# Bucketed attention into a channel mix: row copies on GpSimd's queue, and one written sequence of operations

## The chip, the cores and the metric

The kernel runs on one core of a Trainium2 chip. A core has TensorE (PE in the profile; its weight loads are PEld), VectorE (DVE), ScalarE (ACT), GpSimd (POOL) and SyncE (SP). Each engine works through its own instructions in the order in which they stand in the program, and waits on semaphores for the others; SP here only issues DMAs, which run on 16 DMA engines. "SPq" and "POOLq" in the profile are DMA issues of those queues. The metric is the device time in microseconds, the median of several runs.

## The reference

Two stages follow each other. The first is attention in which a query sees only the keys of its own bucket: a bucket is the pattern of signs of six random projections. The second is a channel mix of the RWKV kind.

```python
batch, n_heads, seq, head_dim = (4, 8, 768, 64)
q_bits = (einsum('bhsd,dk->bhsk', q, proj) > 0)      # proj: 64 x 6
k_bits = (einsum('bhsd,dk->bhsk', k, proj) > 0)
mask = q_bucket[:, :, :, None] == k_bucket[:, :, None, :]
scores = where(mask, q @ k.T / sqrt(64), -1e9)
attn = softmax(scores); x = attn @ v                 # to (batch, 768, 512)
x_prev = x shifted by one position
xk = mu_k * x + (1 - mu_k) * x_prev                  # xr with mu_r
k = relu(xk @ w_k); v = (k * k) @ w_v                # 512 -> 1024 -> 512
out = sigmoid(xr @ w_r) * v
```

All inputs and the output are float32.

## The kernel before, in words

**Tiling.** Two heads make a pair, so there are 16 pairs, four to a batch; after each fourth pair the channel mix of that batch (numbered 0 to 3) can begin. A pair's Q and K are loaded (L485, L491), split by VectorE into an fp16 high part ("hi", L560) and low part ("lo", L563), both in the buffer nh, and transposed by DMA from SP into the operand tile a (L567). Pairs 0 and 1 are instead transposed on TensorE (L638) with evictions by VectorE and ScalarE (L643, L645), piece by piece.

**Bucket bits.** For pairs 1 to 15, TensorE multiplies the tile a with the projections (the "bits" group, 16 matmuls, L586), VectorE turns the signs into fp16 values of fixed size (bx, L589), and four DMAs copy six rows each (Q and K of both heads) back into the tile a, next to the 64 rows of data (L599). After that, one product of the K side and the Q side of a gives the score plus a constant for each bit in agreement, so the exponential of a pair in different buckets vanishes, and no mask is applied. A pair's scores therefore wait for its row copies. Pair 0 writes its bits in place (L668, L670).

**Scores to PV.** A pair has 9 score steps of 1024 columns (L702), each into one of three double banks of PSUM; ScalarE takes the exponential of each (L706). The bits group takes one of the same three double banks. PV is 12 matmuls at a time (L732); VectorE divides (L741 to L748), the result is transposed (L758 or by DMA, L764), and VectorE forms the mixed inputs xk and xr (L789 to L804). V is prepared by GpSimd: copies and sums (L511 to L523).

**Channel mix.** 16 groups with w_k (L822), ScalarE's relu (L826), VectorE's square (L829), 6 groups with w_r (L841) and a tanh (L844), 12 with w_v (L851), the product on VectorE (L858) and the store from SP (L861). w_k is loaded by four DMAs of GpSimd's queue (L446); w_r and w_v are loaded by SP and cast by GpSimd (L470).

**What sets the order.** All of it is added as 1328 operations to a planner (`Plan.add`, L124), each with engine, planned duration and the operations that it depends on. `Plan.schedule` (L159) plays this through in planned time: on each engine, of the operations that are ready, the one with the lowest entry in the list `WANT` (a wanted place for each operation) goes next; a large DMA is held back while the planned DMA work is more than `BACKLOG` ahead; the PSUM banks are given out first free first. What comes out is the fixed order of instructions on each engine; nothing of the plan remains at run time. `LAG` holds the planned time from an engine's end to when another can start.

Of the kernel before, what the change touches and what calls it, by code (L numbers as in the profile page):

```python
# [17 lines left out]
LAG = {"PE": 0.30, "ACT": 0.25, "DVE": 0.20, "POOL": 0.20, "SP": 1.8, "GQ": 2.0}  # L18


BACKLOG = 1.5

# [17 lines left out]
def R(kind, n):  # L40
# [3 lines left out]
WANT = [  # L44
    2, 8, 6, 12, 18, 10, 26, 38, 44, 24, 5, 11, 30, 34, 35, 23, 36, 3, 33, 14, 32, 22, 0, 9,
    25, 1, 39, 42, 45, 48, 49, 46, 59, 31, 112, 84, 74, 63, 101, 324, 348, 401, 425, 387, 414, 455, 482, 379,
    403, 446, 470, 4, 41, 13, 37, 102, 21, 7, 117, 47, 50, 52, 51, 65, 66, 53, 19, 58, 40, 54, 17, 68,
    71, 76, 80, 62, 67, 73, 77, 56, 82, 89, 95, 104, 98, 69, 15, 78, 83, 90, 103, 64, 75, 175, 115, 123,
    135, 133, 61, 57, 72, 87, 28, 27, 70, 60, 96, 86, 100, 79, 29, 20, 55, 16, 107, 110, 134, 120, 127, 119,
    106, 131, 43, 91, 99, 105, 81, 88, 118, 109, 122, 132, 113, 130, 125, 129, 97, 141, 144, 148, 121, 157, 159, 154,  # L50
    161, 155, 166, 167, 170, 176, 179, 181, 188, 185, 108, 85, 221, 137, 147, 152, 156, 94, 92, 128, 93, 126, 114, 158,
    169, 194, 174, 187, 173, 172, 145, 150, 163, 164, 171, 178, 162, 153, 168, 142, 146, 143, 160, 139, 151, 138, 140, 190,
    198, 197, 207, 208, 177, 195, 183, 180, 204, 237, 220, 230, 233, 246, 241, 192, 182, 281, 191, 196, 206, 210, 124, 136,
    149, 111, 116, 165, 186, 193, 227, 202, 228, 211, 214, 184, 257, 262, 231, 238, 239, 244, 219, 217, 226, 218, 189, 200,
    205, 216, 201, 199, 267, 268, 271, 274, 275, 234, 236, 242, 252, 253, 279, 288, 297, 305, 300, 311, 203, 229, 298, 240,
    245, 250, 255, 222, 224, 248, 209, 212, 235, 273, 277, 302, 286, 299, 294, 247, 256, 243, 249, 276, 285, 260, 265, 263,
    269, 283, 295, 251, 270, 278, 290, 225, 215, 315, 292, 280, 291, 318, 293, 296, 307, 319, 323, 330, 334, 338, 341, 345,
    349, 350, 357, 362, 374, 383, 393, 392, 420, 424, 428, 434, 437, 380, 386, 398, 417, 427, 435, 433, 441, 448, 495, 504,
    516, 413, 423, 429, 431, 449, 454, 452, 461, 468, 450, 527, 533, 439, 444, 459, 500, 507, 522, 512, 519, 541, 520, 536,
    539, 485, 492, 525, 546, 550, 597, 497, 514, 558, 563, 566, 607, 542, 560, 562, 567, 572, 638, 578, 586, 594, 649, 616,  # L60
    939, 530, 581, 625, 635, 650, 925, 656, 664, 613, 642, 686, 913, 266, 213, 356, 301, 308, 312, 322, 332, 327, 336, 232,
    223, 259, 254, 258, 272, 284, 304, 329, 328, 343, 316, 346, 352, 333, 344, 351, 360, 325, 335, 339, 408, 317, 331, 310,
    289, 313, 321, 303, 309, 402, 407, 405, 418, 421, 363, 367, 369, 372, 375, 340, 467, 494, 506, 502, 543, 503, 517, 337,
    365, 426, 314, 320, 326, 342, 355, 353, 361, 282, 287, 347, 261, 264, 306, 376, 381, 396, 404, 391, 412, 410, 416, 395,
    406, 399, 411, 359, 368, 422, 430, 388, 397, 354, 373, 384, 390, 370, 378, 471, 475, 508, 490, 524, 457, 462, 469, 473,
    478, 371, 599, 620, 626, 637, 641, 629, 639, 477, 364, 532, 377, 382, 385, 438, 440, 443, 463, 358, 366, 415, 389, 409,
    432, 481, 487, 509, 528, 501, 513, 515, 523, 419, 436, 442, 451, 488, 496, 505, 510, 445, 456, 460, 464, 465, 472, 476,
    480, 529, 535, 499, 545, 547, 583, 585, 593, 602, 606, 466, 612, 628, 633, 647, 655, 644, 678, 484, 511, 553, 447, 453,
    458, 474, 483, 479, 486, 498, 491, 518, 394, 400, 489, 551, 559, 574, 569, 584, 565, 549, 554, 538, 540, 557, 576, 651,
    659, 631, 654, 627, 634, 573, 592, 589, 600, 587, 596, 675, 679, 684, 691, 694, 660, 665, 668, 673, 683, 493, 706, 735,  # L70
    739, 743, 749, 746, 753, 808, 817, 825, 819, 828, 834, 788, 801, 810, 779, 787, 809, 827, 839, 848, 849, 857, 865, 833,
    843, 847, 872, 878, 884, 786, 852, 860, 876, 882, 887, 851, 861, 866, 886, 905, 902, 867, 871, 880, 906, 909, 916, 894,
    897, 901, 864, 908, 911, 783, 797, 923, 935, 953, 1003, 769, 784, 919, 940, 945, 952, 962, 968, 955, 966, 973, 995, 988,
    989, 1035, 1039, 1044, 1049, 999, 1005, 974, 992, 1010, 1017, 1048, 1057, 930, 949, 1061, 1063, 537, 580, 652, 548, 552, 556, 577,
    579, 582, 588, 521, 526, 561, 531, 534, 544, 617, 622, 657, 636, 630, 646, 610, 614, 671, 677, 666, 669, 619, 624, 621,
    632, 604, 609, 648, 653, 601, 605, 640, 645, 693, 713, 715, 718, 721, 688, 701, 704, 708, 710, 590, 772, 793, 794, 796,
    803, 800, 806, 570, 591, 643, 568, 571, 575, 663, 670, 667, 676, 555, 564, 623, 603, 611, 661, 705, 712, 737, 729, 750,
    725, 698, 702, 690, 695, 720, 722, 717, 723, 711, 714, 733, 741, 728, 731, 742, 748, 680, 687, 738, 744, 747, 757, 762,
    758, 752, 767, 771, 773, 681, 781, 812, 814, 821, 831, 818, 836, 618, 755, 917, 672, 682, 685, 696, 699, 703, 707, 595,
    598, 674, 608, 615, 692, 724, 730, 740, 760, 766, 778, 813, 820, 782, 792, 770, 776, 822, 829, 775, 790, 763, 768, 754,  # L80
    764, 751, 756, 761, 777, 856, 842, 841, 858, 862, 798, 802, 815, 823, 826, 709, 895, 915, 920, 921, 927, 924, 1054, 732,
    853, 824, 689, 697, 700, 719, 726, 727, 734, 658, 662, 716, 774, 780, 791, 859, 868, 881, 890, 873, 877, 830, 835, 845,
    850, 869, 874, 883, 891, 879, 885, 795, 804, 855, 863, 837, 846, 805, 811, 899, 918, 934, 937, 938, 893, 896, 898, 910,
    912, 736, 959, 976, 979, 981, 985, 1059, 1066, 1076, 1080, 1085, 1047, 1051, 1071, 1072, 1078, 1082, 1062, 1070, 1075, 1124, 1130, 1134,
    1084, 1090, 1101, 1087, 1093, 1098, 1095, 1108, 1115, 1135, 1141, 1144, 1064, 1106, 1111, 1086, 1100, 1104, 1092, 1120, 1123, 1149, 1156, 1158,
    1131, 1137, 1140, 1119, 1125, 1129, 1112, 1127, 1132, 1154, 1162, 1147, 1187, 1194, 1196, 1146, 1152, 1181, 1185, 1186, 1190, 1193, 1200, 1199,
    1206, 1208, 1211, 1217, 1221, 1161, 1170, 1223, 1227, 1224, 1229, 1232, 1238, 1242, 1246, 1220, 1226, 1235, 1234, 1240, 1243, 765, 807, 816,
    936, 941, 944, 961, 967, 970, 977, 759, 745, 844, 889, 892, 903, 943, 948, 965, 969, 956, 991, 947, 951, 926, 933, 900,
    904, 907, 914, 971, 975, 980, 984, 1004, 1009, 922, 928, 997, 1001, 1007, 1008, 1015, 1019, 1026, 1020, 1023, 1027, 1032, 1036, 983,
    1040, 1053, 1056, 1065, 1069, 1073, 1077, 799, 888, 986, 946, 950, 954, 990, 993, 996, 1000, 785, 789, 832, 838, 840, 854, 958,  # L90
    963, 972, 998, 982, 978, 1011, 1018, 987, 994, 1025, 1028, 1030, 1037, 1034, 1046, 1055, 1068, 1081, 1088, 1089, 1103, 1060, 1067, 1058,
    1094, 1107, 1113, 1117, 1122, 1126, 1128, 1133, 1136, 1002, 1139, 1153, 1155, 1157, 1160, 1159, 1163, 957, 960, 964, 1014, 1024, 1021, 1029,
    870, 875, 929, 931, 932, 942, 1097, 1099, 1105, 1116, 1102, 1110, 1045, 1052, 1013, 1022, 1050, 1074, 1118, 1121, 1091, 1096, 1142, 1145,
    1079, 1083, 1109, 1114, 1143, 1148, 1138, 1150, 1151, 1165, 1164, 1166, 1171, 1174, 1177, 1178, 1031, 1182, 1192, 1195, 1201, 1203, 1198, 1230,
    1006, 1012, 1016, 1033, 1038, 1041, 1042, 1184, 1189, 1197, 1202, 1191, 1188, 1180, 1183, 1173, 1175, 1204, 1207, 1168, 1172, 1176, 1179, 1169,
    1167, 1205, 1209, 1212, 1214, 1216, 1210, 1213, 1215, 1218, 1219, 1043, 1222, 1225, 1228, 1231, 1236, 1239, 1233, 1237, 1250, 1244, 1256, 1245,
    1249, 1251, 1255, 1260, 1262, 1248, 1252, 1254, 1261, 1266, 1268, 1258, 1263, 1265, 1264, 1269, 1271, 1253, 1257, 1259, 1278, 1283, 1286, 1273,
# [5 lines left out]

class Op:
    pass


class Plan:

    def __init__(self, pairs, banks, most, moe_most):
        self.ops = []
        self.writer = {}
# [39 lines left out]
    def schedule(self):  # L159
# [31 lines left out]
        t = 0.0  # L191
# [726 lines left out]
```

## Time and profile before

| | us |
|---|---|
| median of 3 runs (lowest to highest) | 254.8 (254.63 to 255.04) |
| span of the profiled execution, first to last instruction | 249.4 |
| lowest and highest run less that span (the page gives no time around the span) | 5.2 to 5.6 |
| TensorE / VectorE / ScalarE / GpSimd busy | 235.4 / 185.9 / 183.2 / 49.8 |
| first exponential, first matmul of the channel mix, end of TensorE's work | 12.7, 60.8, 245.6 |
| row copies on SP: number x median issue | 60 x 0.693 |

How to read it: a row of the stretches gives, for a window of time, the busy time of each engine in it with the number of instructions. In the order of time a row is a run of equal instructions, with their common length and, in brackets, the idle time of the engine ahead of it and what ended it. The chain of waits is followed back from the last instruction. A busy TensorE is not TensorE at its peak, since the ends of pipelined matmuls are modelled; start-to-start times of matmuls in a run say what they cost.

### The profile page before, as it was taken

What the parts mean: (1) busy time and instruction counts of PE and PEld (TensorE: products, weight loads), DVE (VectorE), ACT (ScalarE), POOL (GpSimd) and SP (SyncE); (2) the same over time, 40 slices, a digit from 0 to 9 for tenths busy, and PEclk for the clock granted to TensorE, in tenths of its full rate; (3) what the DMA queues carried; (4) which work ended last, traced back from release to release, by engine and by line L of the source; (5) the groups of instructions that cost most, each with busy time, mean ns of one, the idle gap of its engine ahead of it and who ended that gap; (6) DMA issues with size and microseconds to landing.
All of it is one profiled execution on the core that took longest, in us unless ns stands there. A gap on an engine that the chain in (4) does not pass through costs nothing.

```text
span 249.4 us, 6171 instructions
## 1 busy us (share of the span) xinstructions
PE 235.4 (94%) x2453; PEld 140.4 (56%) x2453; DVE 185.9 (75%) x415; ACT 183.2 (73%) x242; POOL 49.8 (20%) x89
## 2 busy tenths in 40 slices
PE   7897988897999999999999999999999999999993
PEld 3344654474667555558666666447666666555441
DVE  4997599899986987899989976786856626854321
ACT  3589859869999845899799988169997677247210
POOL 7209142245364123004100000522000000000000
PEclk9799999999999999999999999999999999999999
DMA  7994999998999999989968999945210103220123
GB/s 204 265 314 88 170 277 224 236 231 221 310 216 323 246 266 232 270 235 216 137 206 208 223 215 205 267 74 196 74 42 9 34 9 108 87 84 3 42 84 128
DMA packets 73341, 43.50 MB, mean 174 GB/s; under 512 B 55544, under 2 KB 68192, under 8 KB 73312
## 3 DMA queue, kind: packets, MB, share of 16 engines
q1 hardware_dynamic: 72656, 42.05, 68.8%
q0 software_dynamic: 576, 1.05, 2.3%
q8 instruction: 19, 0.31, 0.5%
q14 instruction: 10, 0.08, 0.1%
q10 hardware_dynamic: 80, 0.00, 0.0%
HBM read 24.12 MB, written 6.29 MB: 122 GB/s over the span
## 4 chain that ended last, share of the span: by engine, by line
PE 77%; DMA 7%; ACT 6%; DVE 3%; SPq 3%; issue 2%; DVEq 0%; ACTq 0%
PE ps_all L702 18%; PE ps_all L851 17%; PE ps_all L822 17%; PE ps_all L732 13%; PE ps_all L841 8%; ACT pt L706 6%; DMA nat<-in_k_dram 5%; PE ps_all L586 3%; DMA a<-bx 3%; SPq L599 2%; DVE bx L589 1%; SPq L567 1%; SPq L491 1%; DVE a L643 1%; DVE nh L625 0%
## 5 line engine op out<-in xcount | busy, mean ns | idle before, releaser
L706 ACT ACTIVATE pt<-ps_all 128x1024 bf16<-128x1024 f32 x144 | 140.6, 1042 | 24.0 <-PE ps_all L702 22.4
L702 PE MATMUL ps_all<-a 128*128 128x512 f16 (+1 forms) x384 | 81.3, 325 | 6.2 <-ACT pt L706 3.5
L702 PEld LDWEIGHTS <-a 128*128 128x128 f16 x384 | 33.6, 97 | 33.1 <-issue 10.4
L732 PEld LDWEIGHTS <-pt 128*128 128x128 bf16 x1152 | 43.6, 97 | 8.5 <-ACT pt L706 0.8
L822 PE MATMUL ps_all<-xk,wk 128*128 128x384 bf16 x256 | 47.4, 326 | 0.0
L851 PE MATMUL ps_all<-wv,k 128*128 128x512 bf16 x192 | 46.8, 379 | 0.0
L732 PE MATMUL ps_all<-va,pt 128*128 128x65 bf16 x1152 | 45.6, 193 | 0.3 <-ACT pt L706 0.2
L826 ACT ACTIVATE kr<-ps_all 128x384 bf16<-128x384 f32 x64 | 30.8, 509 | 7.8 <-PE ps_all L822 4.7
L822 PEld LDWEIGHTS <-wk 128*128 128x128 bf16 x256 | 24.3, 98 | 16.2 <-issue 1.0
L829 DVE TENSOR_TENSOR k<-kr 128x384 bf16<-128x384 bf16 x64 | 22.4, 359 | 14.1 <-ACT kr L826 13.7
L517 POOL TENSOR_TENSOR vt<-vn 128x384 f32<-128x384 f32 x12 | 12.7, 1060 | 90.5 <-DMA vn<-in_v_dram 90.2
L844 ACT ACTIVATE rs<-ps_all 128x512 f32<-128x512 f32 x24 | 14.4, 604 | 22.2 <-PE ps_all L841 15.4
L851 PEld LDWEIGHTS <-k 128*128 128x128 bf16 x192 | 18.4, 98 | 20.1 <-issue 0.3
L858 DVE SCALAR_TENSOR_TENSOR os<-rs,ps_all 128x512 f32<-128x512 f32 x24 | 16.5, 686 | 17.4 <-PE ps_all L851 11.9
L563 DVE SCALAR_TENSOR_TENSOR nh<-nat,nh 128x768 f16<-128x768 f32 x28 | 28.7, 1033 | 0.3
L841 PE MATMUL ps_all<-wr,xr 128*128 128x512 bf16 x96 | 24.5, 379 | 0.0
L560 DVE TENSOR_SCALAR nh<-nat 128x768 f16<-128x768 f32 x28 | 16.3, 583 | 3.9 <-DMA a<-nh 1.5
L748 DVE TENSOR_TENSOR ob<-ps_all,rc 128x384 bf16<-128x384 f32 x32 | 17.7, 554 | 0.7
L589 DVE TENSOR_SCALAR bx<-ps_all 128x768 uint16<-128x768 uint16 x15 | 14.3, 954 | 1.3 <-PE ps_all L586 0.8
L841 PEld LDWEIGHTS <-xr 128*128 128x128 bf16 x96 | 8.8, 98 | 8.8 <-issue 0.3
L586 PE MATMUL ps_all<-a,p 128*32 128x256 f16 (+1 forms) x240 | 13.0, 328 | 0.5 <-DMA a<-nh 0.3
L542 DVE SCALAR_TENSOR_TENSOR va<-ps_all,vn 128x384 bf16<-128x384 f32 x24 | 12.2, 547 | 0.9 <-PE ps_all L537 0.9
(69 smaller groups left out, 157.5 us busy)
## 6 DMA issues: line engine op xcount, KB each, us to landing
vn<-in_v_dram SPq DMA_DIRECT2D x16, 384.0 KB
out_dram<-os SPq DMA_DIRECT2D x24, 256.0 KB
nat<-in_k_dram SPq DMA_DIRECT2D x15, 384.0 KB
nat<-in_q_dram SPq DMA_DIRECT2D x15, 384.0 KB
wk<-in_moe_w_k_dram POOLq DMA_DIRECT2D x4, 256.0 KB, 8.3
wst<-in_moe_w_r_dram SPq DMA_DIRECT2D x2, 512.0 KB
wst<-in_moe_w_v_dram SPq DMA_DIRECT2D x2, 512.0 KB
a<-bx SPq DMA_DIRECT2D x60, 9.0 KB
```

The lines of the kernel that those rows point to most:

```text
L563: nc.vector.scalar_tensor_tensor(out=nh[:, :, D:P], in0=nat.rearrange("p j (c d) -> p (j c) d", d=D), scalar=QS, in1=nh[:, :, 0:D], op0=AL ...
L586: nc.tensor.matmul(ps[32 * i : 32 * i + 32, lo:hi], w_, a_t[sa][:, i, lo:hi], start=st, stop=not st)
L589: nc.vector.tensor_scalar(out=bx_t[sx].bitcast(U16), in0=ps_t[plan.slot[nm]][:, 0:S].bitcast(U16).rearrange("p (c e) -> p c e", e=2)[:, :, 1],
L702: nc.tensor.matmul(ps[:, lo - s * STEP : hi - s * STEP], side_a["k"][sa][:, j, jc * P : (jc + 1) * P], side_a["q"][sa][:, j, q0 : q0 + hi ...
L706: nc.scalar.activation(out=pt_t[sp][:, s * STEP : (s + 1) * STEP], in_=ps_t[plan.slot[nm]], func=AF.Exp, bias=EBIAS, scale=ESC)
L732: nc.tensor.matmul(oo[:, ic * 65 : ic * 65 + 65], pt_t[sp][:, o : o + P], va_t[sa][:, j, jc, 0 : D + 1], start=(not uc and ic == 0 and jc ...
L748: nc.vector.tensor_tensor(out=ob_t[so][:, :, j * D : (j + 1) * D], in0=oo[:, :, 0:D], in1=rc_t[sr][:, 1, :].unsqueeze(2).to_broadcast([P, ...
L822: nc.tensor.matmul(ps[:, 0:HALF], wk_sb[:, d, fc * P : (fc + 1) * P], xk_t[mx[d]][:, h * HALF : (h + 1) * HALF], start=(d == 0), stop=(d = ...
L826: nc.scalar.activation(out=kr_t[sk], in_=sm(nm)[:, 0:HALF], func=AF.Relu, scale=0.5 ** 0.5)
L829: nc.vector.tensor_tensor(out=k2_t[s2][:, h * HALF : (h + 1) * HALF], in0=kr_t[sk], in1=kr_t[sk], op=ALU.mult)
L841: nc.tensor.matmul(sm(nr), xr_t[mx[d]][:, c * P : (c + 1) * P], wr_sb[:, d, :], start=(d == 0), stop=(d == NDC - 1))
L851: nc.tensor.matmul(sm(nv), k2_t[(b * NFC + fc) % NK2][:, c * P : (c + 1) * P], wv_sb[:, fc, :], start=(fc == 0), stop=(fc == NFC - 1))
```

## The change

The four row copies of each of the pairs 1 to 15 are issued by GpSimd on its own DMA queue instead of by SP. The list `WANT` and the readiness rule are gone: a list `ORDER` names all 1328 operations in the sequence in which they are to stand, and `Plan.schedule` only walks through it; it still works out planned times, and takes for an operation that needs PSUM the bank that is planned to come free first. The planned lags and some planned durations differ. In the new sequence, among much else, two of the four w_k loads stand later, the throw-away exponential at L410 stands last, and the tile loads of the first pairs are issued in another order. The operations themselves are the same.

```diff
-LAG = {"PE": 0.30, "ACT": 0.25, "DVE": 0.20, "POOL": 0.20, "SP": 1.8, "GQ": 2.0}
-BACKLOG = 1.5
+LAG = {"PE": 0.21, "ACT": 0.21, "DVE": 0.15, "POOL": 0.18, "SP": 1.8, "GQ": 2.0}
-WANT = [
-    2, 8, 6, 12, 18, 10, 26, 38, 44, 24, 5, 11, 30, 34, 35, 23, 36, 3, 33, 14, 32, 22, 0, 9,
...
+ORDER = [
+    10, 11, 12, 24, 22, 13, 51, 21, 0, 2, 3, 4, 5, 53, 6, 59, 60, 7, 8, 25, 69, 70, 61, 26,
...
+    def sequence(self):
+        if ORDER:
+            return [self.ops[i] for i in ORDER]
...
+        order = self.sequence()
+        for o in order:
+            e = "POOL" if o.eng == "GQ" else o.eng
+            t = max([free[e], o.at] + [self.ops[d].own if self.ops[d].eng == o.eng and not self.ops[d].svc else self.ops[d].vis for d in o.deps])
+            if o.take is not None:
...
+                choices = [(i, (2 * i, 2 * i + 1)) for i in self.pairs] if cls == "sc" else [(b, (b,)) for b in self.banks]
+                choices = [(max(t, *(bank_free[b] for b in bs)), k, i, bs) for k, (i, bs) in enumerate(choices) if not any(used[b] for b in bs)]
+                t, _, self.slot[name], bs = min(choices)
...
-        add(W_CAST[i], {"POOL": 1.06, "ACT": ACT_C(1024), "DVE": DVE_C(1024)}[W_CAST[i]], T + PR["wc"] + X("wc", i), f_c, r=keys,
+        add(W_CAST[i], {"POOL": 1.4, "ACT": ACT_C(1024), "DVE": DVE_C(1024)}[W_CAST[i]], T + PR["wc"] + X("wc", i), f_c, r=keys,
...
-                (nc.scalar if n in ROW_ACT and i % 2 else nc.sync).dma_start(out=a_t[sa][D : D + NB, i, :], in_=bx_t[sx][32 * i : 32 * i + NB, :])
+                nc.gpsimd.dma_start(out=a_t[sa][D : D + NB, i, :], in_=bx_t[sx][32 * i : 32 * i + NB, :])
             w = [("ab", "qk"[i // 2], sa, i % 2, h) for h in range(2)]
-            if n in ROW_ACT and i % 2:
-                add("ACT", 0.45, R("row", n) + 0.01 * i, row, r=[("bx", sx)], w=w, svc=0.17, off=1.15, name=f"row{n}")
-            else:
-                add("SP", 0.76, R("row", n) + 0.01 * i, row, r=[("bx", sx)], w=w, svc=0.17, off=1.15, name=f"row{n}")
+            add("GQ", 0.6, R("row", n) + 0.01 * i, row, r=[("bx", sx)], w=w, svc=0.17, off=1.6, name=f"row{n}")
```

## The prediction

> **What bounds the kernel now.** I read the page's shares first, then busy time in stretches cut at two events (the first softmax exponential at 12.7 us, the first matmul of the channel mix at 60.8), then ScalarE's order of time between them, then what held it.
>
> The page's busy shares, and the stretches (core time, then PE, PEld, DVE, ACT, POOL busy, clock, DMA share, GB/s):
>
> ```profile
> PE 235.4 (94%) x2453; PEld 140.4 (56%) x2453; DVE 185.9 (75%) x415; ACT 183.2 (73%) x242; POOL 49.8 (20%) x89
> ```
>
> ```profile
> 0.00:12.70 12.70, 9.93 (x58) 4.49 (x58) 8.67 (x22) 5.15 (x9) 5.74 (x31) 0.87 0.90 234
> 12.70:60.80 48.10, 41.15 (x542) 25.71 (x540) 41.81 (x71) 40.77 (x44) 19.23 (x23) 1.00 0.92 221
> 60.80:245.60 184.80, 184.36 (x1859) 110.19 (x1857) 134.73 (x324) 137.30 (x190) 24.80 (x36) 1.00 0.66 160
> 245.60:249.40 3.80, 0.00 (x0) 0.00 (x0) 0.68 (x1) 0.00 (x0) 0.00 (x0) 1.00 0.18 70
> ```
>
> After 60.8 TensorE never rests (184.4 of 184.8 us). Before it, nothing is full: TensorE's 41.2 us are ends that are modelled, VectorE and ScalarE have 6.3 and 7.3 us idle. To see what TensorE really needs I add start-to-start times from the chain: a score step 0.43, 12 PV matmuls 0.376, a channel-mix group 0.65 (L822) or 0.863 (L841, L851), a bits group 0.765. That is 144 x 0.43 + 96 x 0.376 + 64 x 0.65 + 72 x 0.863 + 15 x 0.765 + some 9.4 of small groups = 222.7 us. TensorE ends at 245.6, so 22.9 us are lost: 40.5 of the 222.7 lie before 60.8 (20.3 lost there), 182.2 in the 184.8 after it (2.6 lost). So time is to be won before 60.8 alone; after it, only lost.
>
> ScalarE in order of time (start, us, what, and in brackets the idle time ahead):
>
> ```profile
> 12.73 1.94 ACT L706 ACTIVATE pt<-ps_all 128x1024 bf16<-128x1024 f32 x2 [0.33 <-PE ps_all L702]
> ...
> 18.00 9.27 ACT L706 ACTIVATE pt<-ps_all 128x1024 bf16<-128x1024 f32 x10 [0.55 <-DVE mur L436]
> 27.59 1.02 ACT L706 ACTIVATE pt<-ps_all 128x1024 bf16<-128x1024 f32 x1 [0.32 <-PE ps_all L702]
> 29.28 2.85 ACT L706 ACTIVATE pt<-ps_all 128x1024 bf16<-128x1024 f32 x3 [0.66 <-PE ps_all L702]
> 34.74 3.77 ACT L706 ACTIVATE pt<-ps_all 128x1024 bf16<-128x1024 f32 x4 [2.61 <-PE ps_all L702]
> ...
> 54.67 7.44 ACT L706 ACTIVATE pt<-ps_all 128x1024 bf16<-128x1024 f32 x8 [2.14 <-PE ps_all L702]
> ```
>
> An exponential costs 0.93 us in a run (9.27 / 10). The two long pauses stand ahead of pairs 2 and 4. What held the scores there is the bit rows, as the chain shows:
>
> ```profile
> 28.82 0.96 DVE bx L589
> ...
> 32.81 0.45 SPq L491
> 33.30 4.61 DMA a<-bx
> ```
>
> Pair 2's bits were ready at 29.8, but its four copies left SP at 30.1, 30.9, 32.1 and 33.3, between other DMAs, and the last took 4.6 us to land behind two 384 KB loads. One issue costs, by line:
>
> ```profile
> L599 SPq DMA_DIRECT2D a<-bx x60: 658/693/1044, 19.0 to 189.3; - x60
> L446 POOL DMA_DIRECT2D wk<-in_moe_w_k_dram x4: 553/562/759, 5.1 to 6.9; - x4
> ```
>
> **The change part by part.** The program's operations are the same 1328; 60 change queue and nearly all change place.
>
> *Row copies.* SP loses 60 x 0.693 = 41.6 us of issuing, and its transposes, loads and stores no longer stand behind a copy that waits for VectorE's bits (L599 waited 6.1 us for it). GpSimd gains 60 x 0.562 = 33.7 us on 49.8, with a third of the span used: no bound by sum. Queued behind a waiting copy are now GpSimd's V sums (TensorE's PV matmuls wait for those), two of the four w_k loads and the weight casts. After the last of pair 2's copies comes a w_k load; the other stands behind pair 3's copies (due ahead of its first exponential, 17.4 + 23 x 0.94 = 39 by the sums below, so issued by 37); at the slowest landing seen, 10.2 us, it is there by 47, before the channel mix. A small copy on GpSimd's queue is in no row. Its landing is bounded by SP's undelayed copy (2.6 us for the same 9 KB, the chain at 22.91) and by the quickest w_k load (6.9 us for 28 times the bytes). I take 2.6, since size decides the nearer row and the queue is free of 384 KB loads. What issuing on GpSimd does to VectorE: the V work at 18.9 stretched a 0.95 us subtraction to 1.35, the w_k issues at 5.1 to 7.5 stretched none (0.52 to 0.55). I take nothing; the other end is 20 early copies x 0.56 x 0.4 = 4.5 us.
>
> A rule speaks against this step. The four w_k issues, made while VectorE was 88% busy (4.40 of 5 us), took 0.55 to 0.76. In the Trainium skill, page "SBUF — State Buffer", section "SBUF: two separate sides", the descriptors of a DMA issued by GpSimd can't be written while VectorE runs an operation that holds both ports; a later part of the page has 3.1 us beside such an operation against 0.62 alone. As an estimate from that page, four copies would take 12.4 us, 16 would be needed where the gaps given under "After that" have 83 in ten, and the sum would end near 326. I go by the row.
>
> *Order up to the bits of pair 1.* Pair 0's K load now goes second (before: third, landed at 5.83) and VectorE takes its low half early. The first four exponentials come earlier by that, but the scores of the fifth need pair 0's second head, whose bits close a VectorE list. Work is the busy time of VectorE's instructions, taken from this trace and added in the new order. VectorE starts on data at 3.24 as before; up to the end of those bits it has 13.0 us of work, before 13.7 (ended 17.2, so 3.5 idle, nearly all at the start). I take 3.7 idle, one short wait more: 16.7, and with a score step (0.43) and its hand-over the next exponential at 17.4 (before 18.0).
>
> *Bits ahead of the scores.* From bits to first scores of pair 2 TensorE now has 4.8 us of other work (before 4.3), of pair 4 6.0 (4.3); VectorE's list reaches pair 4's bits after 37.5 us of work instead of 41.5. For pair 2: VectorE has its second half split at 15.9 + 3.7 = 19.6, the transpose leaves SP near 20 (before 23.8) and lands near 24, the bits end at 25, VectorE's extraction at 26.3, and the third copy, which the first scores need, lands at 26.3 + 3 x 0.56 + 2.1 = 30. ScalarE finishes pair 1 at 17.4 + 14 x 0.94 = 30.6. The 2.6 us pause goes, so does the 2.1 of pair 4: 32 exponentials from 17.4 end at 47.5, where they ended at 52.5 (and pair 4 began at 54.7).
>
> *The first channel mix* needs the mixed input of pair 3 (xk, L796), and VectorE becomes what is late next: 50.4 us of work stand ahead of its end (before 51.4; xr of pair 2 went behind it), ended at 60.3, thus 8.9 idle. Idle is at least 3.7 and at most the old 8.9; I take 5.0, since the waits for scores that made up most of the rest are gone, but transposes still have to leave its buffers. 50.4 + 5.0 = 55.4; TensorE begins the channel mix at 55.9 and has by its new order done 42.1 us instead of 40.5. Lost by then: 55.9 - 42.1 = 13.8. I add 0.7, since ScalarE, due at pair 4's last PV with 12.8 lost by the same kind of sum, will hardly run without any pause: 14.5 instead of 20.3, **5.8 us gained**.
>
> *After that.* I take the old 2.6 us of loss. Its lower end is 1; upwards the bits tell: from the end of a pair's bits to its first scores TensorE has, for pairs 6 to 15, 6.6, 7.2, 7.5, 11.0, 6.8, 9.2, 8.5, 6.9, 8.4 and 10.9 us of work. With VectorE's turn and extraction (1.6), four issues (2.3) and a landing less its issue (2.0), 5.9 are needed, so all are covered, by 0.7 at the least. If VectorE is 2 us late each time, the closest five fall short by 1.3, 0.7, 0.4, 1.1 and 1.0; upper end 7.
>
> *Small parts.* The activation table was loaded with a throw-away exponential (L410), which now stands last. The load goes to ScalarE's first copy and has no wait of its own, so it lies in the 3 us ahead of the first K load as before; bound: its 1.28. The mu loads go later, read 20 us after. Planned durations and lags change no instruction. At the end the same last matmuls, product and store: 3.8 us.
>
> **Sum.** Span 249.4 - 5.8 = 243.6. The page gives no time around the profiled span; the median of the three runs, 254.8, lies 5.4 above it, which I keep: 249.0.
>
> **The rivals.** (1) *Pauses remain*, 0.18: VectorE keeps its 8.9 us of idle time because other waits replace the old (transposes, V sums behind copies on GpSimd). Lost at the mix 8.3 + 8.9 + 0.5 = 17.7 against 20.3: 2.6 gained, 252.2; with one or two close bits later up to 254.3. For it: SP still waits in order. Against: the rows blamed in the chain are those that move. (2) *GpSimd's queue makes it slower*, 0.14: a copy there costs far more than 0.56 us to issue, VectorE being busy. Place: the bits of the later pairs, where TensorE has no slack. Needed are 3.6 us + 4 issues. At 0.75 each the closest gap is just met; at 1.3, 8.8 are needed, and the ten gaps above fall short by 2.2, 1.6, 1.3, 2.0, 0.3, 1.9 and 0.4, 9.7 in all: 249.0 + 9.7 = 258.7. It decides from about 1.1 us (8.0: 5.0 short in five gaps, and the early pairs late). Against: 0.76 was the most seen. (3) *Better*, 0.08: VectorE idles 3.7 alone, mix at 54.6, later loss 1.5: some 246.6 or less.
>
> **How the numbers follow.** The likeliest case has 0.60: 247 to 251.5, by the ends of idle time and of later loss. The range goes to 245.3 for (3) and to 254.4 for all of (1). A change of 0.2% (0.5 us) is what can be told here. Faster: 0.60 + 0.08 + 0.14 of (1) = 0.82; the same 0.04; slower 0.14.
>
> **What would show it.** ScalarE without pauses over 1 us from 18 to 50 us, the first channel-mix matmul at 55 to 57; row copies on GpSimd at 0.56 to 0.8 us each and landed in 2 to 3; TensorE full after 57. I am wrong if the copies take over 1.1, if VectorE idles over 7 us up to the mix, or if TensorE shows gaps ahead of scores late in the span.

## The result, and the profile after

The changed kernel takes 268.7 us (median of 4 runs, 267.97 to 271.33); the kernel before took 254.9 beside it (254.63 to 257.28). The ratio is 1.055 (95% interval 1.047 to 1.063): it is slower by some 14 us, where I had forecast 249.0 us and a gain. The profiled execution took 268.97 us, 1.8 above its span of 267.2. A kernel now and then runs some per cent slower throughout: the ratios here leave such executions out, the medians don't, and the profiles of e6 and e12 below are of such executions.

The page's busy shares of the changed kernel:

```profile
PE 236.0 (88%) x2435; PEld 140.9 (53%) x2453; DVE 199.3 (75%) x415; ACT 183.4 (69%) x242; POOL 83.6 (31%) x149
```

TensorE and ScalarE do what they did. GpSimd is busy 33.8 us longer, where 33.7 of issuing were forecast (the 60 issues took 31.9). VectorE has 13.4 us more than the 185.9 before, with the same 415 instructions: that was in no term of the sum.

The same stretches, cut at the first exponential (10.2 us) and the first matmul of the channel mix (67.5):

```profile
0.00:10.20 10.20, 7.24 (x40) 3.56 (x41) 5.97 (x15) 4.04 (x7) 4.36 (x22) 1.00 0.82 261
10.20:67.50 57.30, 45.26 (x598) 28.83 (x596) 48.92 (x75) 44.40 (x47) 34.66 (x55) 0.97 1.03 233
67.50:262.80 195.30, 183.49 (x1803) 108.49 (x1819) 143.77 (x327) 134.94 (x188) 44.53 (x72) 1.00 0.60 138
262.80:267.20 4.40, 0.00 (x0) 0.00 (x0) 0.67 (x1) 0.00 (x0) 0.00 (x0) 0.76 0.31 121
```

The mix begins 6.7 us later than before (60.8), not 4.9 earlier, and after it TensorE is no longer full: 183.5 of 195.3 us. By start-to-start times, as in the prediction, 42.1 us of TensorE's need lie before the mix and 180.6 after it, so 25.4 us are lost before it (old: 20.3) and 14.7 after it (old: 2.6). In the middle stretch the DMA share is now 1.03, where the kernel before had 0.92. (The share can pass 1, as it does with 1.49 from 115 to 120 us in the kernel before, so it is no proof by itself that the engines are full.)

ScalarE in order of time (start, us, what, and in brackets the idle time ahead of it):

```profile
27.18 5.61 ACT L640 ACTIVATE pt<-ps_all 128x1024 bf16<-128x1024 f32 x6 [0.68 <-PE ps_all L636]
35.52 1.02 ACT L640 ACTIVATE pt<-ps_all 128x1024 bf16<-128x1024 f32 x1 [2.74 <-PE ps_all L636]
36.77 11.33 ACT L640 ACTIVATE pt<-ps_all 128x1024 bf16<-128x1024 f32 x12 [0.22 <-PE ps_all L636]
49.17 4.69 ACT L640 ACTIVATE pt<-ps_all 128x1024 bf16<-128x1024 f32 x5 [1.07 <-DVE ob L682]
55.47 1.02 ACT L640 ACTIVATE pt<-ps_all 128x1024 bf16<-128x1024 f32 x1 [1.61 <-PE ps_all L636]
```

The pause ahead of pair 2 is there as before, 2.74 us where it was 2.61, and pair 4's exponentials (from 55.47) come in ones, twos and threes. What holds the scores is still the row copies; the copies' own view (issue and landing), then the waits of TensorE's matmuls for them and those of its weight loads, each in the changed kernel first and in the kernel before second:

```profile
L536 POOL DMA_DIRECT2D a<-bx x60: 497/508/809, 19.2 to 191.9; - x60
...
DMA to landing us min/median/max: 1.6/3.8/7.4
```

```profile
PE ps_all L636 <- DMA a<-bx: 8.9, 8, 2.9
```

```profile
PE ps_all L702 <- DMA a<-bx: 1.8, 2, 1.3
```

```profile
PEld L636 <- DMA a<-bx: 7.8, 5, 3.1
```

```profile
PEld L702 <- DMA a<-bx: 2.9, 4, 1.8
```

Issuing is as cheap as forecast, in fact cheaper (0.508 in the median against 0.693 on SP). Landing is not: 3.8 us in the median and up to 7.4. For SP's copies in the kernel before the trace's semaphore counts give 1.84 at the least, 2.74 in the median, 4.94 at most. TensorE's two waits for the copies grew from 1.8 and 2.9 to 8.9 and 7.8. Copy by copy, landing goes with the traffic: of the 60 copies of the changed kernel, the 18 in flight at a DMA share under 0.6 (averaged from issue to landing) landed in 1.8 us in the median, the 27 at 1.0 or more in 5.6. The queues show how such a copy differs on the two paths, after first and before second:

```profile
q1 hardware_dynamic: 71936, 41.50, 66.0%
q0 software_dynamic: 2496, 1.61, 3.1%
```

```profile
q1 hardware_dynamic: 72656, 42.05, 68.8%
q0 software_dynamic: 576, 1.05, 2.3%
```

Sixty copies took 720 packets on SP's path (12 each) and take 1920 on GpSimd's (32 each).

The second cause is on VectorE. Its order of time in the stretch before the mix, and GpSimd's beside it:

```profile
58.95 0.81 DVE L723 TENSOR_TENSOR df<-xt 128x768 bf16<-128x768 bf16 x1
59.80 3.82 DVE L729 SCALAR_TENSOR_TENSOR xk<-df,muk,xt 128x768 bf16<-128x768 bf16 x1
```

```profile
59.81 2.02 POOL L407 CAST wr<-wst 128x1024 bf16<-128x1024 f32 x2
61.79 1.00 POOL L454 TENSOR_TENSOR vt<-vn 128x384 f32<-128x384 f32 x1
62.87 1.02 POOL L457 TENSOR_TENSOR vt<-vt 128x128 f32<-128x128 f32 x1
```

The mixed input xk of pair 2 took 3.82 us; the next one of the same shape, at 66.63 with GpSimd idle, took 1.02. It ended at 63.62, when GpSimd's run of arithmetic, begun at the same moment, was nearly over. GpSimd lost time too: its add at 62.87 took 1.02, where the same add at 58.45 took 0.41. Pair 3's xk, which the channel mix waits for, stands behind it. The Trainium skill, page "SBUF — State Buffer", section "Who interferes with whom", says that a VectorE instruction with two inputs in SBUF contends with a GpSimd instruction that reads SBUF, and that one of them waits; this row agrees, 2.8 us lost in one instruction. I had weighed another rule of that page.

Over the whole run I add up how much each VectorE instruction is longer than the shortest of its kind (same line, operands and shape): 23.9 us after, 11.8 before. After, 32 instructions are more than 0.1 us above the median of their kind, by 17.4 us together; before, 14, by 4.7. Each one of these overlaps an arithmetic instruction of GpSimd; none stands beside DMA issues alone. So it is GpSimd's arithmetic that stretches VectorE, and not the issuing of the copies.

### The profile page after: what moved, and what is told of

Read it like the earlier page. It is cut to its first block, busy times and chain, and to the rows that moved or that the text cites. A ratio compares the mean times of both kernels' runs of the same rounds, so it can differ in the third digit from the quotient of the medians.

```text
span 267.2 us, 6210 instructions
## 1 busy us (share of the span) xinstructions
PE 236.0 (88%) x2435; PEld 140.9 (53%) x2453; DVE 199.3 (75%) x415; ACT 183.4 (69%) x242; POOL 83.6 (31%) x149
## 4 chain that ended last, share of the span: by engine, by line
PE 46%; DVE 20%; DMA 14%; POOL 9%; issue 8%; ACT 1%; SPq 0%; DVEq 0%; POOLq 0%; ACTq 0%
PE ps_all L785 12%; PE ps_all L756 10%; PE ps_all L636 9%; DMA a<-bx 9%; PE ps_all L775 6%; PE ps_all L666 6%; DVE nh L500 4%; POOL a L536 4%; DVE bx L526 2%; PE ps_all L523 2%; DMA a<-nh 2%; DMA nat<-in_k_dram 2%; DMA vn<-in_v_dram 2%; DVE nh L497 2%; POOL vt L454 1%
## 5 line engine op out<-in xcount | busy, mean ns | idle before, releaser
L636 PE MATMUL ps_all<-a 128*128 128x512 f16 (+1 forms) x384 | 81.8, 328 | 12.1 <-DMA a<-bx 8.9
L536 POOL DMA_DIRECT2D a<-bx x60 | 31.6, 532 | 81.7 <-DVE bx L526 56.6
L756 PE MATMUL ps_all<-xk,wk 128*128 128x384 bf16 x256 | 48.0, 326 | 2.5 <-ACT kr L760 1.6
L666 PE MATMUL ps_all<-va,pt 128*128 128x65 bf16 x1152 | 44.6, 194 | 2.8 <-ACT kr L760 2.1
L785 PE MATMUL ps_all<-wv,k 128*128 128x512 bf16 x185 | 44.7, 379 | 0.4
L760 ACT ACTIVATE kr<-ps_all 128x384 bf16<-128x384 f32 x64 | 30.9, 499 | 19.3 <-PE ps_all L756 11.3
L778 ACT ACTIVATE rs<-ps_all 128x512 f32<-128x512 f32 x24 | 14.4, 603 | 27.7 <-PE ps_all L775 25.0
L500 DVE SCALAR_TENSOR_TENSOR nh<-nat,nh 128x768 f16<-128x768 f32 x28 | 31.3, 1120 | 0.6
L775 PE MATMUL ps_all<-wr,xr 128*128 128x512 bf16 x85 | 23.1, 379 | 0.5
L526 DVE TENSOR_SCALAR bx<-ps_all 128x768 uint16<-128x768 uint16 x15 | 14.3, 953 | 10.5 <-PE ps_all L523 10.3
L454 POOL TENSOR_TENSOR vt<-vn 128x384 f32<-128x384 f32 x12 | 12.6, 1050 | 16.8 <-DMA vn<-in_v_dram 16.6
L497 DVE TENSOR_SCALAR nh<-nat 128x768 f16<-128x768 f32 x28 | 17.2, 621 | 0.3 <-DMA nat<-in_k_dram 0.3
(70 smaller groups left out, 180.6 us busy)
```

Of the source, the lines that this page charges most:

```text
L497: nc.vector.tensor_scalar(out=nh[:, :, 0:D], in0=nat.rearrange("p j (c d) -> p (j c) d", d=D), scalar1=QS, scalar2=None, op0=ALU.mult)
L500: nc.vector.scalar_tensor_tensor(out=nh[:, :, D:P], in0=nat.rearrange("p j (c d) -> p (j c) d", d=D), scalar=QS, in1=nh[:, :, 0:D], op0=AL ...
L526: nc.vector.tensor_scalar(out=bx_t[sx].bitcast(U16), in0=ps_t[plan.slot[nm]][:, 0:S].bitcast(U16).rearrange("p (c e) -> p c e", e=2)[:, :, 1],
L536: nc.gpsimd.dma_start(out=a_t[sa][D : D + NB, i, :], in_=bx_t[sx][32 * i : 32 * i + NB, :])
L636: nc.tensor.matmul(ps[:, lo - s * STEP : hi - s * STEP], side_a["k"][sa][:, j, jc * P : (jc + 1) * P], side_a["q"][sa][:, j, q0 : q0 + hi ...
L666: nc.tensor.matmul(oo[:, ic * 65 : ic * 65 + 65], pt_t[sp][:, o : o + P], va_t[sa][:, j, jc, 0 : D + 1], start=(not uc and ic == 0 and jc ...
```

## The experiments

Each kernel differs from one of the two in a few lines. "Old" is the sequence of the kernel before, "new" the written sequence. The kernel before was run beside each batch, with medians from 253.1 to 254.9. Differences between runs of different batches are therefore taken from their ratios to the kernel before of the same batch, times 254.2 us, and come with a 95% range worked out from the two intervals.

**1 to 4: each part alone.** New sequence with the copies on SP (e1), old sequence with the copies on GpSimd (e2), and both sequences without copies (e3 old, e4 new).

```diff
-                nc.gpsimd.dma_start(out=a_t[sa][D : D + NB, i, :], in_=bx_t[sx][32 * i : 32 * i + NB, :])
+                nc.sync.dma_start(out=a_t[sa][D : D + NB, i, :], in_=bx_t[sx][32 * i : 32 * i + NB, :])
```

(e1; in e2 the opposite edit in the kernel before; in e3 and e4 `pass` stands in its place, so the copies are left out and the scores are unmasked.)

> The written order as it stands, with the 60 row copies issued by SP at the same places of the sequence. If GpSimd's queue is what costs (its copies landed in 3.8 us at the median and up to 7.4, where 2.6 was taken), 250 to 256 us, VectorE's busy time back near 186 to 190 us and the first channel-mix matmul near 58 to 61. If it is the order itself, 263 to 269, with the channel mix still at 65 to 68. If both, something between: 257 to 262.

> The order of the kernel before on every engine, with the 60 row copies issued by GpSimd at the places that they had in the whole sequence. If GpSimd's queue is what costs, 261 to 268 us, most of it after 60 us. If it is the order, 253 to 257: the copies then only change queue, and the old order has TensorE work of 4.0 to 13.6 us between bits and first scores.

> The order of the kernel before with the row copies left out (the bits are worked out but not copied, so scores wait for the transposes alone and the output is that of unmasked scores). The floor of what any cheaper copy can bring to the old order: 249 to 252 if the pauses ahead of pairs 2 and 4 are the copies' (4.7 us), under 1 us of gain if other waits take their place.

> The written order with the row copies left out in the same way. If the copies' queue and landing are the whole cause, 244 to 250 us, what the forecast had hoped for from the order or better; if the order itself costs (VectorE stretched beside GpSimd's casts and sums, engines in order behind late operations), 258 to 266.

Measured: e1 317.8 us (ratio 1.245, 1.237 to 1.254), e2 264.9 (1.039, 1.030 to 1.047), e3 251.8 (0.988, 0.981 to 0.996), e4 257.8 (1.012, 1.004 to 1.020). e2 and e3 lie in a range that was expected, e4 just under the upper one.

e1 lies far above all three of its ranges and says nothing of the new sequence by itself: on SP's queue, which runs in order, copies now stand ahead of loads that are needed first. Two of the waits of e1 (us, times, longest), which were 22.4 and 1.2 us at the same places in the kernel before:

```profile
ACT pt L640 <- PE ps_all L636: 60.4, 41, 10.0
...
DVE nh L497 <- DMA nat<-in_k_dram: 19.1, 7, 6.3
```

So the written sequence, as it stands, can't be had without the move. The move can be had without the sequence, and alone costs 10.2 us (e2, against 254.7 beside it), most of it ahead of the mix, which begins at 71.4 instead of 60.8 (expected was a loss after 60 us). The copies as such cost 13.1 us on GpSimd's queue in the old sequence (264.9 - 251.8), 2.9 on SP's (254.7 - 251.8), and 10.9 on GpSimd's in the new one (by the ratios).

e4 is what struck down the forecast's main gain. With no copy at all the new sequence is 6.0 us slower than the old one, and the mix begins at 61.8, not at 55.9. The chain of waits of e4, and VectorE's order of time there:

```profile
20.78 6.30 DMA a<-nh
```

```profile
28.05 0.96 DVE L526 TENSOR_SCALAR bx<-ps_all 128x768 uint16<-128x768 uint16 x1 [4.38 <-PE ps_all L523]
```

The second transpose of pair 2 leaves SP at 20.8, as planned earlier than before, and takes 6.3 us to land. VectorE, which in its new order reaches pair 2's extraction early, stands 4.38 us at it. In the old order it waited 2.50 and 1.31 for PV at that place: one wait has taken the place of others. VectorE's busy and idle time up to the mix (from stretches that end there) is 50.5 + 10.3 us before, 51.4 + 10.4 in e4, 54.9 + 12.6 after.

**5: is it bulk traffic that makes the copies land late?** To e2 I add, at each copy, a small DMA on SP that waits for the same bits and writes to scratch, so that SP is held as it was.

```diff
                 nc.gpsimd.dma_start(out=a_t[sa][D : D + NB, i, :], in_=bx_t[sx][32 * i : 32 * i + NB, :])
+                z = 16 * (4 * (n % 2) + i)
+                nc.sync.dma_start(out=dz[z : z + NB, :], in_=bx_t[sx][32 * i : 32 * i + NB, 0:192])
```

> The old order with the row copies on GpSimd, as in the run before, and besides, at each old place of a row copy in SP's queue, a small copy of the same bits into a scratch tile that nobody reads, so that SP waits for the bits and spends the issue as in the kernel before. If the copies land late on GpSimd's queue because a freed SP sends loads and transposes out beside them, they land in 2.5 to 3 us at the median (SP's own: 2.7) and the time is 254 to 258 us. If it is GpSimd's queue itself (32 packets a copy against 12, completion on all 16 engines, descriptors by software), they stay near 4.2 us and the time at 262 to 267.

Measured: 260.7 us (1.022, 1.014 to 1.031). Sixty DMAs more, and 4.1 us less than e2 (by the ratios, 1.0 to 7.2). The copies on GpSimd's queue now land as SP's did, in e5 first and in e2 second:

```profile
L600 POOL DMA_DIRECT2D a<-bx x60: 499/511/804, 19.9 to 197.8; - x60
...
DMA to landing us min/median/max: 1.6/2.7/4.9
```

```profile
DMA to landing us min/median/max: 1.6/4.2/6.5
```

So the late landing is for the most part not the price of that queue, whose best copy (1.6) is even quicker than SP's (1.84): it comes from the loads and transposes that SP sends while it no longer stands waiting for the bits. A smaller part can be the queue's: over all these runs, copies in flight at a DMA share of 0.8 to 1.0 took 3.3 us in the median from SP (101 copies) and 3.7 from GpSimd (99), and at 1.0 to 1.2, 4.0 (39) and 4.7 (135). The landing came as the first theory had it, the time did not: 260.7 lies between its range and the other's, 5.7 us (3.5 to 7.9) above the kernel before.

**6 and 9: GpSimd's arithmetic beside VectorE.** The V sums are cut to one of 64 columns, in the new sequence without copies (e6) and in the changed kernel (e9).

```diff
-            e.tensor_tensor(out=vt[:, :, :, 0:E], in0=src[:, :, 0:3, 0:E], in1=src[:, :, 3:6, 0:E], op=ALU.add)
+            e.tensor_tensor(out=vt[:, :, :, 0:1], in0=src[:, :, 0:3, 0:1], in1=src[:, :, 3:6, 0:1], op=ALU.add)
...
-            e.tensor_tensor(out=vs[:, :, 0:E], in0=vt[:, :, 0, 0:E], in1=vt[:, :, 2, 0:E], op=ALU.add)
+            e.tensor_tensor(out=vs[:, :, 0:1], in0=vt[:, :, 0, 0:1], in1=vt[:, :, 2, 0:1], op=ALU.add)
```

> The written order without row copies (257.8 us), and GpSimd's V sums cut to one column of 64 or 65 (the sums' buffers are set to one once, so means and the small constant term are wrong; same instructions, same waits, some 20 us less of GpSimd's work). If the order loses because VectorE is stretched beside GpSimd (194.5 us busy against 187.3 in the old order without copies), VectorE falls to 186 to 190 and the time to 250 to 254. If the order loses through late loads and transposes, VectorE falls as well but the time stays at 256 to 258.

> The changed kernel, with the V sums on GpSimd cut to one of 64 columns (their number and their waits stay; part of the computation is left out, as in the run without copies and with narrow V sums). Without copies the same edit took 257.8 to 252.9, that is 4.9 us, and VectorE's busy time from 194.5 to 186.6. Theory A (the cost of the written sequence is VectorE stretched by GpSimd's own arithmetic; the copies' cost is late landing, and the two add up): the same 4.9 us go, 263.8, VectorE busy from 199.3 to about 191, landing of the copies still 3.8 in the median. Theory B (on GpSimd the V sums and the copies also hold each other up, since they stand in one queue): more than 4.9, 257 to 261. Theory C (VectorE is stretched by the issuing of the copies): VectorE's busy time stays above 196, and 266 to 269.

Measured: e6 252.9 us (0.997, 0.993 to 1.001), 3.8 less than e4 by the ratios (1.6 to 6.0); e9 259.9 (1.025, 1.012 to 1.039; its four runs spread from 257.9 to 262.9), 7.6 less than the changed kernel (3.6 to 11.5). The page of e9, and TensorE's waits there:

```profile
PE 233.0 (91%) x2435; PEld 140.2 (55%) x2453; DVE 186.7 (73%) x415; ACT 183.1 (71%) x242; POOL 66.7 (26%) x153
```

```profile
PE ps_all L636 <- DMA a<-bx: 8.8, 8, 2.6
```

VectorE loses 12.6 us of busy time with instructions of its own unchanged, and the mix begins at 62.4 instead of 67.5, though the copies land no earlier (1.6/4.2/7.6) and TensorE's matmuls wait for them as long as before (8.8). The time lies in theory B's range, though the interval reaches up to theory A's 263.8. VectorE's stretch is itself larger with the copies there (12.6 us go, 7.9 without copies). No wait of TensorE's matmuls for GpSimd's V sums shows in the changed kernel (its one wait for GpSimd, 0.2 us, is for a constant), so the sums cost nothing that shows by being late for PV. A share by which V sums ahead of copies delay their issue can't be told apart from the stretch by this run.

**7: the choice of PSUM banks.** The old sequence as `ORDER` in the changed program, copies on SP, so that only the bank given to each operation differs.

```diff
-WANT = [
+ORDER = [0, 22, 25, 51, 17, 10, 2, 57, 1, 23, 3, 11, 53, 9, 4, 56, 19, 21, 15, 5, 24, 12, 33, 20,
...
+        order = self.sequence()
```

> The old sequence of all operations, written out as the new planner's list, with the row copies on SP: only which PSUM bank each operation gets is the new planner's. If banks matter little, within 0.5% of the kernel before (253.5 to 256); if the planner's choice of banks is part of the loss, 257 to 262.

Measured: 254.1 us (0.998, 0.995 to 1.002). In the old sequence the banks don't matter.

**8 and 11: the w_k loads.** e8: the kernel before with its four w_k loads moved behind pair 1's V sums, issued at 21.3 to 23.1 us instead of 5.1 to 6.9. e11: the changed kernel with its two late w_k loads put back beside the two early ones.

```diff
     order = plan.schedule()
+    wg = [o for o in order if o.name.startswith("wg")]
+    order = [o for o in order if o not in wg]
+    at = [o.name for o in order].index("vsum1c") + 1
+    order[at:at] = wg
```

> The kernel before with its four w_k loads moved on GpSimd's queue from its start to behind the V sums of pair 1 (some 25 us in). If the DMA engines bound the first 60 us, the first loads land sooner, the first exponential comes 1 to 3 us earlier and the time falls to 251 to 254; if the pauses come from row copies alone, 254 to 255.5.

> The changed kernel with its four w_k loads together at the place of the first of them, as in the kernel before (issued at 5 to 8 us instead of two of them near 29 and 43). Moving all four to 21 to 23 us in the kernel before cost 7 us. Theory A (1 MB in the stretch in which the DMA engines are full delays what TensorE needs): half of that comes back, 264 to 267, the first channel-mix matmul at 64 to 66 instead of 67.5. Theory B (two loads spread apart are hidden): 268 to 270, mix still at 67 to 68; then the early loads may also delay the first K and Q loads, which shows in the first exponential after 10.2.

Measured: e8 261.3 us (1.029, 1.025 to 1.033), outside both ranges, and the first exponential came at 13.9, later and not earlier. The loads themselves landed soon enough; pair 1's second exponential came at 29.0 instead of 23.4 and the mix at 69.0 instead of 60.8. TensorE's matmuls waited for row copies on SP's own queue, 6.5 us where the kernel before had 1.8:

```profile
PE ps_all L702 <- DMA a<-bx: 6.5, 4, 4.1
```

Four loads of 256 KB put into the busy stretch cost 7 us, without anything waiting for them. e11: 270.9 us (1.070, 1.062 to 1.077), above both ranges and no better than the changed kernel, mix at 68.6, first exponential at 10.2 as in the changed kernel. Two such loads spread far apart cost nothing that shows; I had held it possible that half of e8's loss would come back (and had put the two loads at 1 MB, where they are 0.5).

**10, 13, 14, 15: are the two causes separate?** V sums of one column in the old sequence: copies on GpSimd (e10), no copies (e13), copies on GpSimd with the small ones on SP (e14), and copies on SP (e15). The edits are those shown.

> The old sequence with the copies on GpSimd's queue, and the V sums cut to one of 64 columns (part of the computation left out). With full V sums it took 264.9. Theory A (its cost is the late landing of the copies alone; 4.2 of its 10 us came back when SP was held at the old places): 263 to 265, landing still 4 in the median. Theory B (the V sums that stand behind waiting copies make PV late, and that is the rest that holding SP did not bring back): 259 to 262, with TensorE's waits for the copies (11.2 and 11.2 us) unchanged.

> The old sequence without the copies and with V sums of one column (both left out as before). The run without copies had 251.8 us, VectorE 187.3 us busy. Theory A (in the old sequence GpSimd's V sums stretch VectorE little, so the 3.2 us that narrow V sums gave with the copies on GpSimd are an effect of the two together): 251 to 252, VectorE busy 184 to 186. Theory B (V sums cost the old sequence 3 us whatever the copies do): 248 to 249.

> The old sequence, copies on GpSimd, small copies on SP at the old places, V sums of one column. With full V sums 260.7; without the SP copies and with narrow V sums 261.7. Theory A (late landing by bulk transfers, 4.2 us, and V work beside VectorE, 3.2 us, are separate and add up): 257 to 258, landing 2.7 in the median, the first channel-mix matmul at 64 to 65. Theory B (they are the same microseconds, since a late copy is what puts V work beside VectorE): 260 to 261.

> The kernel before with V sums of one column (part of the computation left out). Theory A (with copies on SP the V sums are hidden): 253.5 to 254.5, VectorE busy from 185.9 to 184 or so. Theory B (they cost 3 us in any sequence): 251 to 252.

Measured, with all the pairs in one table (median in us; VectorE busy in brackets; difference by the ratios, with its 95% range):

| sequence, copies | V sums as they are | of one column | difference |
|---|---|---|---|
| old, none (e3, e13) | 251.8 (187.3) | 249.4 (184.0) | 0.9, -1.7 to 3.4 (3.3) |
| old, SP (before, e15) | 254.2 (185.9) | 252.7 (184.2) | 0.4, -0.8 to 1.6 (1.7) |
| old, GpSimd and small ones on SP (e5, e14) | 260.7 (188.7) | 256.3 (183.5) | 2.9, 0.3 to 5.5 (5.2) |
| old, GpSimd (e2, e10) | 264.9 (192.9) | 261.7 (187.8) | 1.4, -1.5 to 4.3 (5.1) |
| new, none (e4, e6) | 257.8 (194.5) | 252.9 (186.6) | 3.8, 1.6 to 6.0 (7.9) |
| new, GpSimd (after, e9) | 268.7 (199.3) | 259.9 (186.7) | 7.6, 3.6 to 11.5 (12.6) |

Wherever VectorE is less stretched, the time falls, by a quarter to six tenths of it; in three of the six pairs the fall is clear of the noise. e14 answers the open question: holding SP gives 4.1 us with full V sums (1.0 to 7.2) and 5.6 with narrow ones (3.3 to 8.0), so the late landing and the stretch show as separate costs. (e14's landing median was 3.3, though, not the 2.7 that was expected, and its time is below both of its theories.) e10's time lies in the range of its theory B, but its gain is not clear of noise, and no wait of TensorE for the V sums shows in e2. e13 lies between its two theories. e15 is not told apart from the kernel before: with the copies on SP the V sums cost at most 1.6 us.

Of the 14.0 us between the kernel before and the changed one (11.9 to 16.0), 7.2 are V sums beside VectorE (7.6 - 0.4; 3.1 to 11.3), and 6.8 remain with narrow ones (e15 to e9; 3.2 to 10.4).

**12: is it the spacing of SP's issues, or its waiting?** The changed kernel, and beside each copy a DMA on SP from a constant, which waits for nothing.

```diff
                 nc.gpsimd.dma_start(out=a_t[sa][D : D + NB, i, :], in_=bx_t[sx][32 * i : 32 * i + NB, :])
+                z = 16 * (4 * (n % 2) + i)
+                nc.sync.dma_start(out=dz[z : z + NB, :], in_=idh[32 * i : 32 * i + NB, :])
```

> The changed kernel, and beside each copy on GpSimd a small DMA on SP at the same place of the sequence, from a constant to scratch, which waits for nothing: SP keeps its 60 issues of some 0.6 us, but not the waits for bits. Theory A (what the old SP copies did was to space the bulk loads and transposes by their issue time): landing of the copies falls from 3.8 to 3.2 or less, and 3 to 5 us come back: 264 to 266. Theory B (it is SP's standing still for the bits that kept bulk transfers away from the copies): landing stays 3.6 to 4, and 268 to 271, as SP's own work only gets later.

Measured: ratio 1.071 (1.057 to 1.084), landing 1.6/3.5/8.7, its median between those of the two theories, the time above theory A's range. SP's own issue time spaces nothing that helps. With e5 this leaves SP's standing still until the bits were there as what kept bulk transfers away from the copies; in the new sequence that hold was not run.

**What no run separates: the clock.** TensorE's granted clock falls to half for 3.4 us, or twice that, at a time in these traces. Ahead of the mix that happens, for 3.4 us each, once in the kernel before (8.4 to 11.8) and once in the changed one, four times in e2, twice in e5 and never in e9. Between the kernel before and the changed one it therefore makes no difference there. The stretch of the changed kernel, with the 3.4 us ahead of it:

```profile
53.50:56.90 3.40, 1.34 (x18) 0.97 (x19) 2.02 (x4) 1.38 (x2) 3.13 (x6) 1.00 1.07 343
56.90:60.30 3.40, 3.40 (x25) 2.04 (x23) 2.25 (x4) 2.53 (x3) 3.23 (x6) 0.50 1.26 201
```

In the 3.4 us ahead of each of these eight, TensorE was at most 0.6 busy, though other stretches as idle passed without one. So a wait of TensorE may be paid a second time in slower matmuls, by at most 1.7 us a stretch as an estimate (half of 3.4). For e2 that is up to 5 us more than the kernel before has, so what e5 wins back need not be landing time alone.

## Why the prediction was wrong

In the sum's own terms: 10.9 us more were lost before the mix than forecast (25.4 against 14.5), 12.1 more after it (14.7 against 2.6) and 0.6 at the end, less 3.6 that were too many between span and time. That takes 249.0 to the 269.0 of the profiled execution. Two terms failed above all: the landing of a copy, taken as 2.6 us (measured 3.8 in the median, up to 7.4), and "I take nothing" for what GpSimd does to VectorE (13.4 us more busy). A third, VectorE's idle time up to the mix, was to fall to 5.0 us and did not fall.

*What bounds the kernel.* Right for the kernel before (time lost before 60.8, TensorE full after it). The same rows held what was missed: a DMA share of 0.92 in that stretch, which I showed and did not price. e8 shows that more traffic there costs time. The 5.4 us kept between span and time were a mixed term: in the later runs the profiled execution lies 1.8 above its span, so the execution whose profile I read was probably of some 251.2 us, quicker than the three runs shown.

*Row copies, issue.* Right: 0.51 us against 0.562 taken, 0.81 at most. The rule of the Trainium skill, page "SBUF — State Buffer", section "SBUF: two separate sides", on blocked descriptors, with the 3.1 us of the page, showed in no issue here, with VectorE 75% busy.

*Row copies, landing.* Wrong term: 2.6 taken, 3.8 measured in the median and 7.4 at most. The bounds were 2.6 and 6.9, and the lower one was taken. "The queue is free of 384 KB loads" was true and beside the point: the copies landed late whenever the DMA engines were busy with the loads of the other queue (1.8 us at a share under 0.6, 5.6 at 1.0 or more). For pair 2 the copies left GpSimd from 28.0 on (extraction ended at 27.7, forecast 26.3) and took 5.1 to 5.9 us, so the scores came at 34.8, not 30. SP, which I had freed, made the traffic (e5).

*What GpSimd does to VectorE.* Wrong term: "I take nothing", other end 4.5. Measured 13.4 us over the span, 4.4 of it before the mix. My bound counted only the issuing; the overlaps in the trace, e6 and e9 put the loss beside GpSimd's arithmetic, which the new sequence and the later copies moved beside VectorE's long operations.

*Order up to the bits of pair 1.* Wrong, if by little: the bits of pair 0's second head ended at 17.96 (16.7 forecast, 17.2 before), and the fifth exponential, which needs them, came at 18.65 (17.4 forecast, 18.0 before). The first exponentials came 2.5 us earlier, the fourth already 0.7 later, and nothing followed from the gain.

*First channel mix.* Wrong even without copies: VectorE's idle time was to fall from 8.9 to 5.0; by the stretches it stayed (10.3 and 10.4 in e4), because pair 2's second transpose landed in 6.3 us instead of 4 and VectorE then waited at the extraction. "Transposes still have to leave its buffers" named the wait, but priced it at one us.

*After that.* Old loss of 2.6 taken, upper end 7; 14.7 measured. The 2.6 was that of a quick execution: e7, the old sequence in a profiled execution of 255.9 us, loses 6.6 there (188.8 us for 182.2 of need). Without copies the new sequence already loses 9.7 there (TensorE's work ends at 252.1, 190.3 us after the mix begins, for 180.6 of need), and 4.5 of the 6.1 us in which TensorE stands idle lie up to 95 us. The stretch of e4 by its columns, and TensorE's longest wait in it:

```profile
61.80:95.00 33.20, 28.70 (x299) 18.16 (x300) 29.07 (x56) 25.85 (x37) 10.10 (x11) 0.95 1.01 259
```

```profile
90.76 0.87 PE L756 MATMUL ps_all<-xk,wk 128*128 128x384 bf16 x4 [2.79 <-ACT kr L760]
```

The chain of waits leads from there back through VectorE's work from 79.2 us on. VectorE is 88% busy in this stretch, but it is 87% busy in e3 (60.2 to 95.0), where TensorE idles for 0.8 us only, so a busy VectorE alone is not the reason; what in the new sequence is, was not tried. The remaining 5 us came with the copies, whose waits after 67.5 are 4.1 us of matmuls and 3.8 of weight loads.

*The rivals.* (1) was right that the idle time stays (8.9 in its words) but ended at 252 to 254, with the copies costing nothing. (2) came out with the right sign, by a cause that I had not given it: not issues of over 1.1 us (the longest was 0.81), but their landing. That its price of 9.7 us late in the span was near what was lost there is luck, and its 258.7 still lies 10 us too low.

What stays open: with narrow V sums and no copies the new sequence is still 3.0 us behind the old one (e6 and e13 by the ratios, 1.2 to 4.9). VectorE's wait at pair 2's extraction is the likely part of it, argued from e4 and not tried. In the old sequence, e14, with SP held and narrow V sums, is still 3.2 us (1.4 to 4.9) behind e15; whether that is the 60 small DMAs added, the queue or the clock was not tried. A GpSimd order with the V sums of a pair ahead of copies that wait for bits was not run either, since its buffers are loaded too late for that.

## What to carry to other kernels

An engine that stands waiting in order can be what keeps bulk transfers away from small urgent ones; before freeing its queue, look at the share of the DMA engines in that stretch, and if it is as high as here (0.92 before, 1.03 after), price the urgent transfer by the slow landings and not by the quick ones. Work put on GpSimd is not free because GpSimd is idle: look which VectorE operations it will stand beside, and add up their lengths over the shortest of their kind. A forecast for a new order should also name the wait that takes the place of each one removed, with the landing time of the transfer behind it.

## What was not expected of the hardware

A 9 KB copy between two places in SBUF lands in 1.6 us from GpSimd's queue at best, quicker than 1.84 from SP's, because it costs less to issue (0.508 against 0.693 us in the median); from the end of the issue the best are alike (1.10 and 1.14). At the same traffic it is the slower one (4.7 against 4.0 us in the median at a DMA share of 1.0 to 1.2), and it takes 32 packets instead of 12. One VectorE instruction of 1.02 us can take 3.82 when GpSimd works through several operations in a row beside it.
